# Decode attention with a squared-ReLU MLP: w1 loaded after the last V, some w2 rows on five DMA engines, wo in mid-step

## The chip, the cores and the metric

The kernel runs on one core of a Trainium2 chip. The time is device microseconds of one execution; 8 runs of the kernel before have a median of 137.36 us.

## The reference

Two tokens (one of each of two sequences) pass in parallel through an attention over the last 2048 positions of a cache and through an MLP; both results are added to the input. All arrays are bf16.

```python
# B=2, Sq=1, D=576, Hq=32, Hkv=16, Sk=8192, Dh=128, F=4608
def _A_ref(x, k_cache, v_cache, wq, wo):        # W = 2048, rep = 2
    q = (x @ wq).reshape(B, Sq, Hq, Dh).transpose(0, 2, 1, 3)
    k = jnp.repeat(k_cache[:, :, Sk - W:, :], rep, axis=1)
    v = jnp.repeat(v_cache[:, :, Sk - W:, :], rep, axis=1)
    scores = jnp.einsum("bhqd,bhkd->bhqk", q, k) * (Dh ** -0.5)
    o = jnp.einsum("bhqk,bhkd->bhqd", softmax(scores), v)
    return o.transpose(0, 2, 1, 3).reshape(B, Sq, Hq * Dh) @ wo

def _B_ref(x, w1, b1, w2, b2):
    h = x @ w1 + b1
    r = jnp.where(h > 0, h, 0)
    return (r * r) @ w2 + b2

xn = layernorm(x)
out = x + _A_ref(xn, ...) + _B_ref(xn, ...)
```

## The kernel before

**Units.** The attention is cut into NU = 8 units. A unit is one sequence and TH = 4 K/V heads, that is NC = 8 query heads. Its K is one tile of 128 partitions x 16 KB (2.1 MB), and so is its V. Units 2t and 2t+1 are the two sequences of head group t, of which there are NQ = 4.

**A step of a unit** (`step`): TensorE transposes K in NG = 8 groups of eight 128x128 blocks (`transposes`, L237); ScalarE and VectorE copy the groups to SBUF in turn (L240, L242); TensorE multiplies them with q (`scores`, L252). In the same loop go the products of the probabilities of the unit two back with its V (`pv`, L289). Then `softmax` works on VectorE, POOL and ScalarE: the maximum over columns and, by a reduction of POOL, over partitions, the exponential, the sums. When both units of a head group have their PV, `wo_proj` at the end of the step spreads the result (`rr`, on VectorE), gathers it with 8 selection matmuls (`wps`, L306), copies it (`ws`) and adds 16 matmuls with wo to the output sum `out_ps`, a PSUM tile that takes all contributions to the result (`out_acc`, L213: two matmuls of 288 columns for each row of weights).

**The MLP.** h is computed transposed: w1 is the stationary operand, 36 column chunks of 128 for each of KC = 5 row blocks (`mlp_h_block`, L323). The columns of a chunk are FR = 18 apart, so that w2 can be loaded with 18 whole rows of 1152 B behind each other on a partition. A bias and the square (L327, L331) give `hT_sb`; `mlp_o` multiplies it with one row of w2 per partition at a time into `out_ps`. Before, `mlp_h_block` runs in the steps of units 1 and 2, and `mlp_o` at the very end.

**Loads.** x comes over ScalarE's queue, b1 and b2 over POOL's (L146, L148), all else over SP's in the order in which the program lists it: wq with K0 between, k1, two tiles of w1, v0, k2, the rest of w1, v1, wo0, k3, then in turn V and K of later units with a wo tile for each head group, and last w2 in the five pieces of `W2P`, 9, 9, 9, 6 and 3 rows. K, V and w2 share a pool of six buffers (`kvpool`), so a load waits until what used the buffer six tiles earlier is done with it. w1 takes the four wide buffers of wq; wo has two buffers. `out_ps` is opened with x and b2 ahead of all other matmuls but the transposes.

**The end.** After the last piece of w2, `out_ps` is copied (L414) and stored from SP and ScalarE.

Of the kernel before, what the change touches and what calls it, by code (L numbers as in the profile page):

```python
# [9 lines left out]
BF16 = mybir.dt.bfloat16  # L10
# [6 lines left out]
def kernel(  # L17
# [43 lines left out]
    FR = L1 // P  # L61
    NFC = S * FR
    OH = D // 2
# [47 lines left out]

    def w_operands(tiles, c, col0, L, step=1):
        last = col0 + (P - 1) * step
        if c < NFULL:
            return tiles[c][:, col0:last + 1:step], c
        sg = col0 // L
        assert last // L == sg
        return tiles[c][:, col0 - sg * L:last - sg * L + 1:step], NFULL + sg
# [6 lines left out]

    def issue_w2(s, r0, r1):
        tl = kvpool.tile([P, (r1 - r0) * D], BF16, tag="kv", name=f"w2_{s}_{r0}")
        rows = B_w2[s * L1:(s + 1) * L1, :].rearrange("(p r) n -> p (r n)", r=FR)
        nc.sync.dma_start(out=tl[:], in_=rows[:, r0 * D:r1 * D])
        w2_tiles[(s, r0)] = tl  # L130

    x_sb = const.tile([B, D], BF16, name="x_sb")
# [10 lines left out]
    for c in range(2, KC):  # L143
        issue_wq(c)
    b1_sb = const.tile([P, S, FR], BF16, name="b1_sb")
    nc.gpsimd.dma_start(out=b1_sb[:], in_=B_b1.rearrange("(s p r) -> p s r", s=S, p=P))  # L146
    b2_sb = const.tile([1, D], BF16, name="b2_sb")
    nc.gpsimd.dma_start(out=b2_sb[:], in_=B_b2.rearrange("(o n) -> o n", o=1))  # L148

    ones_f = const.tile([P, P], F32, name="ones_f")  # L150
# [60 lines left out]
    def out_acc(lhsT, rhs_of, start=False, stop=False):  # L211
        for i in range(2):
            nc.tensor.matmul(out_ps[32 * i:32 * i + B, :], lhsT=lhsT, rhs=rhs_of(i * OH, (i + 1) * OH),  # L213
                             start=start, stop=stop, skip_group_check=True)

    out_acc(ident[:B, :B], lambda a, z: x_sb[:, a:z], start=True)
    out_acc(ones_b[:, :], lambda a, z: b2_sb[:, a:z])

# [77 lines left out]

    def wo_proj(tq):
        oG = oG_tiles.pop(tq)
# [9 lines left out]
        ws = work.tile([P, WR, B], BF16, tag="ws", name=f"ws_{tq}")  # L308
        nc.vector.tensor_copy(out=ws[:], in_=wps[:])  # L309
        wo_sb = wo_tiles.pop(tq)  # L310
        for r in range(WR):
# [4 lines left out]
    def mlp_h_block(c):  # L316
        if c == 0:
            mlp["ps"] = psum.tile([P, NFC, B], F32, tag="misc", bufs=2, name="hT_ps")
        hT_ps = mlp["ps"]
        for s in range(S):  # L320
            for r in range(FR):
                lhsT, xc = w_operands(w1_tiles, c, s * L1 + r, L1, FR)
                nc.tensor.matmul(hT_ps[:, s * FR + r, :], lhsT=lhsT, rhs=xnT[:, xc, :],  # L323
                                 start=(c == 0 and s == 0 and r == 0), stop=(c == KC - 1), skip_group_check=True)
        if c == KC - 1:
            t1 = work.tile([P, NFC, B], F32, tag="t1", name="t1")
            nc.vector.tensor_tensor(out=t1[:], in0=hT_ps[:],  # L327
                                    in1=b1_sb[:].rearrange("p s r -> p (s r)").unsqueeze(2).to_broadcast([P, NFC, B]),
                                    op=ALU.add)
# [5 lines left out]
    def mlp_o(s, r0, r1, last=False):  # L335
        w2_sb = w2_tiles.pop((s, r0))
        for r in range(r0, r1):
            o = (r - r0) * D
            out_acc(mlp["h"][:, s * FR + r, :], lambda a, z: w2_sb[:, o + a:o + z], stop=(last and r == r1 - 1))

    def load_k(u):
        for f in issue_kv(k_tiles, A_k_cache, u, "k"):
            f()

    def load_v(u):
        for f in issue_kv(v_tiles, A_v_cache, u, "v"):
            f()

    W2P = [(0, 0, 9), (0, 9, 18), (1, 0, 9), (1, 9, 15), (1, 15, 18)]

    load_k(1)
    issue_w1(0)
    issue_w1(1)
    load_v(0)
    load_k(2)
    for c in range(2, KC):
        issue_w1(c)
    load_v(1)
    issue_wo(0)
    load_k(3)  # L360
    nxt = {0: [], 1: [], 2: [lambda: load_v(2), lambda: load_k(4)]}

    def step(u, extra=()):
        for g in range(NG + 2):
            if g < NG:
                transposes(u, g)
            if u >= 1 and 1 <= g <= NG:
                if u >= 2:
                    pv(u - 2, g - 1)
            if g >= 2:  # L370
                scores(u, g - 2)
        softmax(u)

# [10 lines left out]
    softmax(0)  # L384
    step(1)
    mlp_h_block(0)
    mlp_h_block(1)
    for u in range(2, NU + 2):
        if u < NU:
            step(u)  # L390
        else:
            for g in range(NG):
                pv(u - 2, g)
        if u == 2:
            for c in range(2, KC):
                mlp_h_block(c)
        if u - 2 >= 1 and (u - 2) % B == B - 1:
            wo_proj((u - 2) // B)
        if u < NU:
            load_v(u)  # L400
            if u % B == 0:
                issue_wo(u // B)
            if u + 2 < NU:
                load_k(u + 2)
        if u >= NU - 1:
            pass
        if u == NU - 1:
            for w in W2P:
                issue_w2(*w)
    for i, w in enumerate(W2P):  # L410
        mlp_o(*w, last=(i == len(W2P) - 1))

# [34 lines left out]
```

## Time and profile before

| | |
|---|---|
| median of 8 runs | 137.36 us (137.16 to 137.5) |
| the profiled execution | 137.44 us, span of its instructions 135.6 us |
| TensorE matmuls, weight loads | busy 101.2 us (75%), 92.2 us (68%), 2054 of each |
| VectorE, ScalarE, POOL | busy 53.8, 43.0, 10.0 us |
| mean granted TensorE clock | 0.786 of full |
| read from HBM | 53.62 MB, 395 GB/s over the span |
| K transposes | 512 matmuls, 264 ns listed each |
| scores, PV | 512 each, 168 and 167 ns listed |
| h, 36 chunks x 5 blocks | 180 matmuls, 201 ns listed |

A busy share is the time in which an engine has an instruction in hand. TensorE's matmuls overlap, so the listed time of one is longer than the distance to the next, and the share says little about how close it is to its limit. The line of tenths for DMA gives the mean share of the 16 DMA engines that were moving data in each fortieth of the span. A wait is put down to what ended it last.

### The profile page before, as it was taken

What the parts mean: (1) busy time and instruction counts of PE and PEld (TensorE: products, weight loads), DVE (VectorE), ACT (ScalarE), POOL (GpSimd) and SP (SyncE); (2) the same over time, 40 slices, a digit from 0 to 9 for tenths busy, and PEclk for the clock granted to TensorE, in tenths of its full rate; (3) what the DMA queues carried; (4) which work ended last, traced back from release to release, by engine and by line L of the source; (5) the groups of instructions that cost most, each with busy time, mean ns of one, the idle gap of its engine ahead of it and who ended that gap; (6) DMA issues with size and microseconds to landing.
All of it is one profiled execution on the core that took longest, in us unless ns stands there. A gap on an engine that the chain in (4) does not pass through costs nothing.

```text
span 135.6 us, 4461 instructions
## 1 busy us (share of the span) xinstructions
PE 101.2 (75%) x2054; PEld 92.2 (68%) x2054; DVE 53.8 (40%) x124; ACT 43.0 (32%) x47; POOL 10.0 (7%) x31
## 2 busy tenths in 40 slices
PE   1049928599968999679943995998399599768661
PEld 0039927589968999639943994798399489754430
DVE  7502511574352433502553446365544654650001
ACT  6704730165013801005601550362155137110000
POOL 6400000110110001100011001101100110110000
PEclk9999995559955995555995599599559959955999
DMA  4999999999999999999999999999999999999940
GB/s 109 423 421 425 423 435 413 417 440 421 430 404 419 440 413 413 441 425 408 437 425 430 416 435 420 410 435 425 430 430 413 437 411 427 413 416 413 390 161 1
DMA packets 5278, 53.90 MB, mean 397 GB/s; under 512 B 630, under 2 KB 652, under 8 KB 1164
## 3 DMA queue, kind: packets, MB, share of 16 engines
q1 hardware_dynamic: 5188, 53.61, 94.6%
q8 instruction: 16, 0.26, 0.8%
q0 software_dynamic: 64, 0.01, 0.1%
q14 instruction: 2, 0.02, 0.0%
q10 hardware_dynamic: 8, 0.00, 0.0%
HBM read 53.62 MB, written 0.00 MB: 395 GB/s over the span
## 4 chain that ended last, share of the span: by engine, by line
DMA 70%; PE 23%; issue 1%; DVE 1%; POOL 1%; ACT 1%; POOLq 0%; ACTq 0%
DMA k<-in_A_k_cache_dram 44%; DMA w<-in_B_w_dram 22%; PE kT_ps L237 14%; DMA b_sb<-in_B_b_dram 4%; PE sc_ps L252 3%; PE oT_ps L289 3%; PE out_ps L213 2%; PE qT_ps L225 1%; ACT kT L240 1%; POOL b_sb L146 1%; DVE sub L266 1%; DVE fin_sb L414 0%; POOL gmax L262 0%; PE pro_ps L186 0%; DVE gm L264 0%
## 5 line engine op out<-in xcount | busy, mean ns | idle before, releaser
L237 PE MATMUL kT_ps<-ident,k 128*128 128x128 bf16 x512 | 48.6, 264 | 10.2 <-DMA k<-in_A_k_cache_dram 10.0
L237 PEld LDWEIGHTS <-k 128*128 128x128 bf16 x512 | 40.5, 121 | 12.1 <-DMA k<-in_A_k_cache_dram 10.9
L240 ACT COPY kT<-kT_ps 128x1024 bf16<-128x1024 bf16 x32 | 32.3, 1012 | 40.0 <-PE kT_ps L237 40.0
L242 DVE COPY kT<-kT_ps 128x1024 bf16<-128x1024 bf16 x32 | 22.1, 690 | 33.1 <-PE kT_ps L237 33.1
L252 PE MATMUL sc_ps<-qT_all,kT 128*128 128x8 bf16 x512 | 21.7, 168 | 1.3 <-ACT kT L240 0.6
L252 PEld LDWEIGHTS <-kT 128*128 128x128 bf16 x512 | 19.4, 101 | 2.1 <-ACT kT L240 0.8
L289 PE MATMUL oT_ps<-pT,v 128*128 128x8 bf16 x512 | 15.4, 167 | 1.5 <-ACT pT L269 0.9
L269 ACT ACTIVATE pT<-sub 128x512 bf16<-128x512 f32 x8 | 5.0, 630 | 35.3 <-DVE sub L266 35.3
L289 PEld LDWEIGHTS <-v 128*128 128x128 bf16 x512 | 14.4, 99 | 1.7 <-DMA v<-in_A_v_cache_dram 0.9
L271 DVE TENSOR_REDUCE l<-pT 128x8 f32<-128x512 bf16 x8 | 8.5, 1064 | 4.5 <-ACT pT L269 4.5
L323 PE MATMUL hT_ps<-xnT,w 128*128 128x2 bf16 x144 | 9.8, 201 | 0.0
L323 PEld LDWEIGHTS <-w 128*128 128x128 bf16 x144 | 9.4, 167 | 0.0
L258 DVE TENSOR_REDUCE m<-sc_ps 128x8 f32<-128x512 f32 x8 | 5.5, 691 | 9.7 <-PE sc_ps L252 9.7
L262 POOL PARTITION_ALL_REDUCE gmax<-m x8 | 2.9, 365 | 84.9 <-DVE m L260 84.9
L213 PE MATMUL out_ps<-wo,ws 128*2 128x288 bf16 x64 | 7.2, 392 | 2.4 <-DVE ws L309 2.4
L213 PE MATMUL out_ps<-w,hT_sb 128*2 128x288 bf16 x72 | 5.7, 308 | 2.4 <-DMA w<-in_B_w_dram 2.4
L213 PEld LDWEIGHTS <-hT_sb 128*2 128x2 bf16 x72 | 3.4, 91 | 4.8 <-issue 3.0
L213 PEld LDWEIGHTS <-ws 128*2 128x2 bf16 x64 | 3.1, 103 | 4.8 <-DVE ws L309 2.8
L225 PE MATMUL qT_ps<-xnT,wq 128*128 128x2 bf16 x128 | 3.9, 164 | 2.8 <-DMA wq<-in_A_wq_dram 2.5
L225 PEld LDWEIGHTS <-wq 128*128 128x128 bf16 x128 | 3.7, 99 | 2.8 <-DMA wq<-in_A_wq_dram 2.6
L266 DVE TENSOR_TENSOR sub<-sc_ps,gm 128x512 f32<-128x512 f32 x8 | 5.5, 690 | 0.3
L273 POOL PARTITION_ALL_REDUCE lsum<-l x8 | 3.2, 398 | 24.5 <-DVE l L271 24.5
(58 smaller groups left out, 35.3 us busy)
## 6 DMA issues: line engine op xcount, KB each, us to landing
v<-in_A_v_cache_dram SPq DMA_DIRECT2D x8, 2048.0 KB, 28.5
k<-in_A_k_cache_dram SPq DMA_DIRECT2D x7, 2048.0 KB, 29.4
w<-in_B_w_dram SPq DMA_DIRECT2D x4, 1152.0 KB, 17.6
wo<-in_A_wo_dram SPq DMA_DIRECT2D x4, 1152.0 KB, 27.3
wq<-in_A_wq_dram SPq DMA_DIRECT2D x4, 1024.0 KB, 7.0
w<-in_B_w_dram SPq DMA_DIRECT2D x3, 1296.0 KB, 22.3
k<-in_A_k_cache_dram SPq DMA_DIRECT2D x2, 1024.0 KB, 9.1
w<-in_B_w_dram SPq DMA_DIRECT2D x1, 864.0 KB, 15.7
```

Of the source, the lines that this page charges most:

```text
L213: nc.tensor.matmul(out_ps[32 * i:32 * i + B, :], lhsT=lhsT, rhs=rhs_of(i * OH, (i + 1) * OH), start=start, stop=stop, skip_group_check=True)
L225: nc.tensor.matmul(qT_ps[:, h, :], lhsT=lhsT, rhs=xnT[:, xc, :], start=(c == 0 and h == 0), stop=(c == KC - 1), skip_group_check=True)
L237: nc.tensor.transpose(out=kT_ps[:, i * P:(i + 1) * P], in_=k_sb[:, j * Dh:(j + 1) * Dh], identity=ident[:])
L240: nc.scalar.copy(out=kT[:], in_=kT_ps[:])
L242: nc.vector.tensor_copy(out=kT[:], in_=kT_ps[:])
L252: nc.tensor.matmul(sc_ps[:, g * JG + i, :], lhsT=kT[:, i * P:(i + 1) * P], rhs=qT_all[:, b, tq * NC:(tq + 1) * NC], start=True, stop=True)
L258: nc.vector.tensor_reduce(out=m1[:], in_=sc_ps[:].rearrange("p j c -> p c j"), axis=AX.X, op=ALU.max)
L266: nc.vector.tensor_tensor(out=sub[:], in0=sc_ps[:], in1=gm2[:].unsqueeze(1).to_broadcast([P, NJ, NC]), op=ALU.subtract)
L269: nc.scalar.activation(out=pT[:], in_=sub[:], func=ACT.Exp, scale=scale)
L271: nc.vector.tensor_reduce(out=l1[:], in_=pT[:].rearrange("p j c -> p c j"), axis=AX.X, op=ALU.add)
L289: nc.tensor.matmul(oT_ps[:], lhsT=v_sb[:, j * Dh:(j + 1) * Dh], rhs=pT_tiles[u][:, j, :], start=(j == 0), stop=(j == NJ - 1))
L323: nc.tensor.matmul(hT_ps[:, s * FR + r, :], lhsT=lhsT, rhs=xnT[:, xc, :], start=(c == 0 and s == 0 and r == 0), stop=(c == KC - 1), skip_g ...
```

## The change

- `FT`, `FX`, `CH`: the second half of w2's rows is no longer 18 rows on each of 128 partitions. 16 rows on each stay so (2048 rows); 240 rows go to a tile of 20 partitions x 12 rows, `w2x_sb`, and 16 rows to a tile of 16 partitions x 1 row, `w2y_sb`. h has 47 chunks in place of 36: 34 of 128 columns, 12 of 20 and one of 16. `hT_ps` is set to zero first.
- `issue_w2x`: `w2x_sb` is loaded by four loads of five partitions (13,824 B each), one after another of the first four among the loads v1, k3, v2, k4, with `w2y_sb` behind the fourth.
- b1 is loaded in four parts into a zeroed tile, b1 and b2 are issued on POOL after unit 0's softmax, and x and b2 are added to `out_ps` after step 1.
- Order of SP's loads from k1 on: v0, k2, v1, wo0, k3, v2, k4, wo1, v3, k5, v4, k6, v5, k7, wo2, v6, v7, w1 (two tiles), wo3, w1 (three tiles), w2.
- `wo_proj` is cut into `wo_sel` and `wo_acc`. For head groups 0 and 1 they run inside the steps of units 4 and 6, at groups 3 and 6. For the last two they run between the PVs of the last units and the h blocks.
- All of h is computed after the last PV, then the 13 rows of `w2x_sb` and `w2y_sb` (`mlp_x`), then w2 in pieces of 9, 9, 9, 4, 2 and 1 rows.

```diff
+    XR, XP, XE = 12, 20, 5
+    FT = (L1 - XR * XP) // P
+    FX = L1 - FT * P
+    XQ = FX - XR * XP
+    FX0 = L1 + FT * P
+    CH = [(r, FR, P) for r in range(FR)] + [(L1 + r, FT, P) for r in range(FT)]
+    CH += [(FX0 + r, XR, XP) for r in range(XR)] + [(FX0 + XR * XP, 1, XQ)]
+    NFC = len(CH)
...
+        nr = FT if s else FR
         tl = kvpool.tile([P, (r1 - r0) * D], BF16, tag="kv", name=f"w2_{s}_{r0}")
-        rows = B_w2[s * L1:(s + 1) * L1, :].rearrange("(p r) n -> p (r n)", r=FR)
+        rows = B_w2[s * L1:s * L1 + nr * P, :].rearrange("(p r) n -> p (r n)", r=nr)
...
+    w2x_sb = const.tile([XP, XR * D], BF16, name="w2x_sb")
+    w2y_sb = const.tile([XQ, D], BF16, name="w2y_sb")
+    x_parts = list(range(XP // XE))
+
+    def issue_w2x():
+        if x_parts:
+            i = x_parts.pop(0)
+            rows = B_w2[FX0:FX0 + XR * XP, :].rearrange("(e i r) n -> i e (r n)", e=XE, r=XR)
+            nc.sync.dma_start(out=w2x_sb[i:XP:XP // XE, :], in_=rows[i])
+            if not x_parts:
+                nc.sync.dma_start(out=w2y_sb[:], in_=B_w2[FX0 + XR * XP:F, :])
...
-    def wo_proj(tq):
+    wo_state = {}
+
+    def wo_sel(tq):
...
+        wo_state[tq] = ws
+
+    def wo_acc(tq):
+        ws = wo_state.pop(tq)
         wo_sb = wo_tiles.pop(tq)
...
+            nc.vector.memset(mlp["ps"][:], 0.0)
         hT_ps = mlp["ps"]
...
+        for i, (f0, step, m) in enumerate(CH):
+            lhsT, xc = w_operands(w1_tiles, c, f0, L1, step, m)
+            nc.tensor.matmul(hT_ps[0:m, i, :], lhsT=lhsT, rhs=xnT[:, xc, :],
+                             start=(c == 0 and i == 0), stop=(c == KC - 1), skip_group_check=True)
...
+    def mlp_x():
+        for i, (f0, step, m) in enumerate(CH[FR + FT:]):
+            w = w2x_sb[0:m, i * D:(i + 1) * D] if m == XP else w2y_sb[:]
+            out_acc(mlp["h"][0:m, FR + FT + i, :], lambda a, z: w[:, a:z])
+
     def load_k(u):
...
+        if u >= 3:
+            issue_w2x()
 
     def load_v(u):
...
+        if u >= 1:
+            issue_w2x()
+
+    W2P = [(0, 0, 9), (0, 9, 18), (1, 0, 9), (1, 9, 13), (1, 13, 15), (1, 15, 16)]
 
     load_k(1)
-    issue_w1(0)
-    issue_w1(1)
     load_v(0)
     load_k(2)
-    for c in range(2, KC):
-        issue_w1(c)
     load_v(1)
     issue_wo(0)
     load_k(3)
...
-    step(1)
+    load_v(2)
+    b1_sb = const.tile([P, NFC], BF16, name="b1_sb")
+    nc.gpsimd.memset(b1_sb[:], 0.0)
+    o = 0
+    for f0, n, m in ((0, FR, P), (L1, FT, P), (FX0, XR, XP), (FX0 + XR * XP, 1, XQ)):
+        nc.gpsimd.dma_start(out=b1_sb[0:m, o:o + n], in_=B_b1[f0:f0 + n * m].rearrange("(p r) -> p r", r=n))
+        o += n
+    b2_sb = const.tile([1, D], BF16, name="b2_sb")
+    nc.gpsimd.dma_start(out=b2_sb[:], in_=B_b2.rearrange("(o n) -> o n", o=1))
+    step(1, {})
+    load_k(4)
+    issue_wo(1)
+    out_acc(ident[:B, :B], lambda a, z: x_sb[:, a:z], start=True)
+    out_acc(ones_b[:, :], lambda a, z: b2_sb[:, a:z])
+    for u in range(2, NU):
+        hooks = {}
+        if u >= 4 and u % B == 0:
+            hooks = {3: [lambda t=u // B - 2: wo_sel(t)], 6: [lambda t=u // B - 2: wo_acc(t)]}
+        step(u, hooks)
+        if u + 1 < NU - 1:
+            load_v(u + 1)
+        if u + 3 < NU:
+            load_k(u + 3)
+        if u == 4:
+            issue_wo(2)
+        if u == 5:
+            load_v(NU - 1)
+            issue_w1(0)
+            issue_w1(1)
+        if u == 6:
+            issue_wo(3)
+            for c in range(2, KC):
+                issue_w1(c)
+            for w in W2P[:2]:
+                issue_w2(*w)
+    for w in W2P[2:4]:
+        issue_w2(*w)
+    for g in range(NG):
+        pv(NU - 2, g)
+    issue_w2(*W2P[4])
+    wo_sel(NQ - 2)
+    wo_acc(NQ - 2)
+    for g in range(NG):
+        pv(NU - 1, g)
+    issue_w2(*W2P[5])
     mlp_h_block(0)
     mlp_h_block(1)
...
+    wo_sel(NQ - 1)
+    wo_acc(NQ - 1)
+    for c in range(2, KC):
+        mlp_h_block(c)
+    mlp_x()
+    for i in range(len(W2P)):
+        mlp_o(*W2P[i], last=(i == len(W2P) - 1))
```

## The prediction

> **What bounds the kernel now.** I read the busy slices and the DMA queues of the page first, because a kernel that reads 53.6 MB for two tokens is most likely bound by its loads.
>
> ```profile
> DMA  4999999999999999999999999999999999999940
> ...
> q1 hardware_dynamic: 5188, 53.61, 94.6%
> q8 instruction: 16, 0.26, 0.8%
> ```
>
> The 16 DMA engines are full in nearly every slice, and queue q1, which holds all the loads that SP issues, is 94.6% of what they do. The q8 line will matter: 16 packets of 16 KB, which carry instructions. The table by stage shows where the engines stop being full.
>
> ```profile
> core 0: us, PE busy (x) PEld busy (x) DVE busy (x) ACT busy (x) POOL busy (x), PEclk, DMA share, GB/s
> ...
> 60.00:90.00 30.00, 23.91 (x469) 22.23 (x466) 13.12 (x26) 11.38 (x12) 1.53 (x4) 0.75 1.01 424
> 90.00:119.00 29.00, 23.87 (x546) 22.46 (x544) 15.15 (x32) 11.38 (x12) 1.89 (x5) 0.82 1.01 423
> 119.00:128.00 9.00, 7.08 (x124) 4.84 (x125) 2.04 (x7) 0.63 (x1) 0.40 (x1) 0.62 1.00 414
> 128.00:129.50 1.50, 0.34 (x6) 0.26 (x7) 0.00 (x0) 0.00 (x0) 0.00 (x0) 1.00 0.72 293
> 129.50:131.40 1.90, 1.08 (x20) 0.63 (x16) 0.00 (x0) 0.00 (x0) 0.00 (x0) 1.00 0.50 189
> 131.40:132.00 0.60, 0.60 (x12) 0.41 (x9) 0.00 (x0) 0.00 (x0) 0.00 (x0) 1.00 0.12 46
> ```
>
> The DMA share is 1.0 until 128 us. Then it is 0.50 for 1.9 us: **half of the engines have nothing left, the other half still work.** The packet records of the trace say the same. The last piece of w2 is marked done by eight engines between 128.2 and 129.5, and by the other eight between 131.4 and 131.8. Following each engine from load to load by the moments of its marks, I see it lose about 1.55 us at once when one of the 16 instruction packets falls on it. They fall on eight engines in turn, twice each: 2 x 1.55 = 3.1 us, the gap between the groups. The late eight set the end. The timeline shows what is behind them.
>
> ```profile
> 131.25 0.90 PE L213 MATMUL out_ps<-w,hT_sb 128*2 128x288 bf16 x12 [0.82 <-DMA w<-in_B_w_dram]
> ...
> 132.34 0.53 PE L213 MATMUL out_ps<-w,hT_sb 128*2 128x288 bf16 x6 [0.18 <-DMA w<-in_B_w_dram]
> ...
> 132.91 0.45 DVE L414 CAST fin_sb<-out_ps 34x288 bf16<-34x288 f32 x1 [10.06 <-PE out_ps L213]
> 133.38 0.32 SPq L415 DMA_DIRECT2D out_dram<-fin_sb  x1
> ```
>
> The last w2 piece lands at 132.3 us, its three rows take 0.53 us, then come a copy and the store. Only two things can move the end: when the last engine is done, and how much TensorE work follows the last landing.
>
> [...] The kernel before has only 128-row loads on SP, so its trace doesn't test the case of five. [...]
>
> **The change, part by part.**
>
> *Rows of w2 on five engines.* 256 of the rows leave the even split: 256 x 1152 B / 16 = 18,432 B less on each engine. The load of 16 rows puts 1,152 B back: 17,280 B less. At 424 GB/s (stage 60 to 90 us), 26.5 GB/s an engine, that is **-0.65 us**[...]. The other 240 rows, 276,480 B, come in four loads of five partitions: 55,296 B[...], net +38,016 B, **+1.43 us** there.
>
> *Smaller pieces.* The last w2 loads go from 6 and 3 rows to 4, 2 and 1: nine more packets per engine, counting the 16-row load. In the packet records 6912 B took 264 ns and 3456 B 139 ns, which leaves some 10 ns a packet beyond the bytes: +0.09 us. b1 comes in four small loads in place of one. Before, one packet of 576 B per engine took some 40 ns, and its mark 9 ns; three more loads and their marks are 0.05 to 0.15 us, I take +0.10.
>
> *The tail.* One row follows the last landing in place of three. The trace has the rows of this stage 122 ns apart at full clock: two rows less are **-0.24 us**, if TensorE is waiting for that landing and its clock is up (at half clock rows are 240 ns apart, as before 126.0 us, and the single row costs 0.12 more).
>
> *w1 behind the last V.* The bytes are the same, so this costs nothing as long as the queue never runs dry and TensorE is done with everything else when the last pieces land. K and V of a unit are 4.19 MB, 9.9 us at 424 GB/s. TensorE's step of unit 6, from its K at 97.2 to its last PV at 106.3, took 9.1 us, so it keeps up by 0.8 us a unit. Behind k7 there will be wo2, v6, v7, w1, wo3 and w2, 16.9 MB: k7 lands 40 us before the end of the stream, at about 92, and v7 at about 104.5. Scores and softmax of unit 7 (4.7 us from first reduction to reciprocal, at 116.7 to 121.4 before) let PV of unit 7 end near 107. The one-row load waits for that, since it takes v7's buffer, and its turn comes near 130: 20 us of cover.
>
> The h blocks are tighter. By the bytes behind them, w1's third and fourth tiles land at 115.8 and 118.6, its rest at 120.0, the three w2 pieces of nine rows at 123.1, 126.3 and 129.4, the last row at 131.8. In the trace the h matmuls start 62 ns apart at either clock; the 13 new chunks have 20 or 16 columns in place of 128, and I price them at the 27 ns of wq's matmuls (32 in 0.79 to 0.99 us). A block is 34 x 62 + 13 x 27 ns = 2.5 us, the last ends at 123.5, bias and square at 124.1. Then come 47 rows. They start at half clock, since the clock stood at 0.5 through the h blocks at 51 to 54 us. It rose after 3.1 us of rows before (122.9 to 126.0); its changes lie 3.4 us or a multiple apart, so 1.9 to 5.3 us until it rises are possible. All rows together take 47 x 0.122 + 0.49 x that time: without any waiting they end between 130.8 and 132.4, at 131.6 in the middle. The landing allows 132.0. **The cover is 0.4 us in the middle case, and -0.4 in the worst**; I take 0.
>
> *Work moved or added elsewhere, taken at zero.* The 55 more matmuls for h and 22 more for the output, in that reckoning already, are 154 more instructions with their weight loads[...]. wo in mid-step removes waits of about 2 us each (1.1 for rr, 1.0 for ws) from TensorE, which then waits for K instead. The last two wo projections lie between 104 and 114 us, before w1 is complete. The new VectorE memset (0.30 us for out_ps) lies there too. POOL gets a memset and five loads at 0.56 to 1.02 us behind the sum of softmax 0; the next POOL work, the maximum of unit 1, comes after a K that lands at 25.8 us and a step. b2 may land near 37 us, with step 2 of TensorE queued behind its matmul, whose K comes at about 36: a delay of a microsecond, which the 0.8 us a unit and the buffers take up. SP issues five more loads at about 0.4 us each. In the trace an SP load from the ninth on never goes out before the eighth ahead of it has landed (v1 at 25.83, k1 at 25.82). Counting that in the new order, at least 5.4 MB, 12.7 us, stay in flight.
>
> **The sum**: late engines -0.65 + 0.09 + 0.10 = -0.46; tail -0.24; together -0.70. The profiled execution took 137.44 us (span 135.60 and 1.84 around it), so 136.74; the median of the runs is 0.08 lower: **136.7**. The five engines end at 128.2 to 129.5 plus 1.62, at most 131.1; the late ones at 131.8 - 0.46 = 131.3. They still set the end, if the five are free ones.
>
> [...] No record bears an engine's number. [...] I take three in four for free.
>
> **The rivals.** *A hit engine is among the five* (0.16, slower). Its mark, 131.4 to 131.8, moves by 1.43 + 0.19 to 133.0 to 133.4, 1.2 to 1.6 later than the latest before; less the tail, +1.0 to +1.4: about 138.5. It decides from the point where one of the five had a mark before above 130.4, and all of the late group do. *TensorE is late for the last pieces* (0.14): a late rise of the clock costs 0.4; if the narrow chunks take 62 ns too, blocks of 2.9 us follow each other without a gap from 115.8 and end 1.0 later; both together +1.4. That gives 137.1 to 138.1, middle 137.5: from faster through none to slower. Against it stands the middle case's cover. *The small loads go to all engines* (0.06, no difference): then tail and packets remain, -0.24 + 0.19, 137.3.
>
> **How the numbers follow.** Forecast 0.64, all of it faster; rivals 0.16, 0.14, 0.06. What a measurement of this kernel can tell from no change is about 0.2%, 0.27 us. Of the late TensorE I count 0.05 faster, 0.04 same, 0.05 slower: faster 0.69, same 0.10, slower 0.21. The bounds of the forecast's terms give 136.4 to 137.0. Idle time of the early eight is worth at most 8 x 3 / 16 = 1.5 us with full levelling, which with the tail would be 135.6; I set the low end at 136.0 for a part of that. The high end, 138.0, takes in the second and third rivals and leaves out the first, which with some low cases is under 2 in 10.
>
> **What will show it.** In the profile after: a share of the DMA engines above 0.8 until a microsecond before the last landing (right), or a stretch near 0.3 or less with a few at work (the first rival); the last w2 landing at about 131.8; two matmuls after it; TensorE waiting for w2 before the last pieces (if it never waits, the second rival); DMA share at 1.0 from 2 to 128 us, or the queue ran dry. I am wrong on the main step if the last landing doesn't come earlier than 132.3.

## The result and the profile after

The changed kernel takes 143.14 us (median of 11 runs, 141.02 to 145.58) where the kernel before takes 137.37: the ratio is 1.0347, with an interval of 1.0322 to 1.0372. By that ratio it is slower by 4.8 us, where 0.7 us less was forecast. Medians here and below are of all runs, while ratios, and differences between kernels, compare the runs within 1.5% of the fastest of their kernel (for the changed kernel five of them, median 142.28 us, for e17 only two). The changed kernel scatters far more than the kernel before, which keeps to 137.2 to 137.6 at clocks from 0.74 to 0.79. Its profiled execution is the longest of all (146.17 us, span 144.1) and has the lowest mean TensorE clock, 0.692, so its times late in the span are a bad case; e7 below has the same instructions in a profile of 141.38 us.

The busy slices and DMA queues of the page, after:

```profile
PEclk9999975579655555955985557975896555555569
DMA  4999999999999999999999999999999999992000
...
q1 hardware_dynamic: 5404, 53.61, 88.9%
q8 instruction: 16, 0.26, 0.7%
```

The loads did what was forecast. There are again 16 instruction packets. The last w2 load gives 16 landing signals in both profiles (between its two groups of eight before, the DMA share is 0.50, so each is read as one engine's): before, eight came from 128.9 to 129.9 us and eight from 131.9 to 132.29; after, three came from 128.2 to 128.9 and thirteen from 130.0 to 131.85. But for three engines the two groups have closed up, and the last landing is 0.44 us earlier. But the row of tenths has three empty slices behind it: for some 12 us the kernel runs on with no load left. The table by stage (engine columns in the order PE, PEld, DVE, ACT, POOL, then PEclk, DMA share, GB/s) shows who runs:

```profile
114.00:131.00 17.00, 16.00 (x259) 15.15 (x258) 1.01 (x5) 0.00 (x0) 0.00 (x0) 0.50 0.96 397
131.00:134.30 3.30, 3.25 (x28) 1.49 (x30) 0.00 (x0) 0.00 (x0) 0.00 (x0) 0.50 0.02 8
134.30:141.20 6.90, 6.88 (x70) 3.85 (x68) 0.00 (x0) 0.00 (x0) 0.00 (x0) 0.62 0.00 0
```

TensorE is busy with hardly a pause, at half clock nearly throughout. Its timeline from the last PVs on, after:

```profile
104.70 1.75 PE L301 MATMUL oT_ps<-pT,v 128*128 128x8 bf16 x64
106.30 0.35 PE L320 MATMUL wps<-rr,sel 128*128 128x16 bf16 x8
109.94 2.08 PE L228 MATMUL out_ps<-wo,ws 128*2 128x288 bf16 x16 [3.28 <-DVE ws L323]
111.96 1.87 PE L301 MATMUL oT_ps<-pT,v 128*128 128x8 bf16 x64
...
114.62 5.51 PE L341 MATMUL hT_ps<-xnT,w 128*128 128x2 bf16 x92
...
127.58 2.83 PE L341 MATMUL hT_ps<-xnT,w_rem 128*128 128x2 bf16 x47
131.05 3.04 PE L228 MATMUL out_ps<-w2x_sb,hT_sb 20*2 20x288 bf16 x24 [0.64 <-DVE hT_sb L349]
133.89 0.44 PE L228 MATMUL out_ps<-w2y_sb,hT_sb 16*2 16x288 bf16 x2
134.26 6.92 PE L228 MATMUL out_ps<-w,hT_sb 128*2 128x288 bf16 x68
```

Before, the three last groups of rows each waited for w2; two of them stand in the prediction, and this is the first:

```profile
129.16 1.27 PE L213 MATMUL out_ps<-w,hT_sb 128*2 128x288 bf16 x18 [1.40 <-DMA w<-in_B_w_dram]
```

After, no row waits for any load: **TensorE sets the end, by itself.** Two things stand out. The first is the wait of 3.28 us ahead of the rows of wo 2, with PV of unit 7 queued behind it. VectorE's timeline says what the copy `ws` was waiting for:

```profile
104.88 0.69 DVE L270 TENSOR_REDUCE m<-sc_ps 128x8 f32<-128x512 f32 x1 [0.45 <-PE sc_ps L264]
...
107.92 1.05 DVE L283 TENSOR_REDUCE l<-pT 128x8 f32<-128x512 bf16 x1 [0.69 <-ACT pT L281]
109.57 0.20 DVE L287 RECIPROCAL rinv<-lsum 128x8 f32<-128x8 f32 x1 [0.60 <-POOL lsum L285]
109.69 0.12 DVE L306 TENSOR_TENSOR oG<-oT_ps,rinv 128x8 bf16<-128x8 f32 x1
109.72 0.16 DVE L323 CAST ws<-wps 128x16 bf16<-128x16 f32 x1
```

The copy takes 0.16 us, but it stands behind the whole softmax of unit 7, with its waits for POOL and ScalarE. It is not the only one: `ws` of wo 0, in step 4, waits behind softmax 3 in the same way, for 3.62 us. The second is that 13 narrow rows (20 or 16 partitions) run at 0.24 us each, and that the clock rises only at 139.6 us, 8.5 us after the first row.

### The profile page after: what moved, and what is told of

Read it like the earlier page. It is cut to its first block, busy times and chain, and to the rows that moved or that the text cites. A ratio compares the mean times of both kernels' runs of the same rounds, so it can differ in the third digit from the quotient of the medians.

```text
span 144.1 us, 4625 instructions
## 1 busy us (share of the span) xinstructions
PE 112.6 (78%) x2131; PEld 99.4 (69%) x2131; DVE 53.2 (37%) x125; ACT 42.4 (29%) x47; POOL 11.4 (8%) x35
## 4 chain that ended last, share of the span: by engine, by line
PE 56%; DVE 16%; DMA 12%; ACT 5%; issue 4%; POOL 3%; SPq 2%; POOLq 0%; ACTq 0%
PE kT_ps L249 18%; PE out_ps L228 13%; DMA wq_rem<-in_A_wq_dram 12%; PE hT_ps L341 9%; PE sc_ps L264 9%; PE oT_ps L301 6%; DVE l L283 4%; DVE sub L278 3%; ACT pT L281 3%; ACT kT L252 2%; DVE kT L254 2%; DVE m L270 2%; POOL gmax L274 2%; SPq L107 1%; POOL lsum L285 1%
## 5 line engine op out<-in xcount | busy, mean ns | idle before, releaser
L249 PE MATMUL kT_ps<-ident,k 128*128 128x128 bf16 x512 | 51.3, 272 | 3.8 <-DMA k<-in_A_k_cache_dram 2.4
L249 PEld LDWEIGHTS <-k 128*128 128x128 bf16 x512 | 42.1, 124 | 4.2 <-DMA k<-in_A_k_cache_dram 2.5
L254 DVE COPY kT<-kT_ps 128x1024 bf16<-128x1024 bf16 x32 | 21.6, 682 | 24.0 <-PE kT_ps L249 24.0
L301 PE MATMUL oT_ps<-pT,v 128*128 128x8 bf16 x512 | 16.2, 167 | 1.2 <-issue 1.2
L228 PE MATMUL out_ps<-wo,ws 128*2 128x288 bf16 x64 | 8.4, 439 | 6.9 <-DVE ws L323 6.9
L341 PEld LDWEIGHTS <-w 128*128 128x128 bf16 (+2 forms) x188 | 10.9, 153 | 0.6 <-issue 0.5
L341 PE MATMUL hT_ps<-xnT,w 128*128 128x2 bf16 (+2 forms) x188 | 11.2, 194 | 0.0
L228 PEld LDWEIGHTS <-ws 128*2 128x2 bf16 x64 | 4.1, 115 | 9.2 <-DVE ws L323 7.1
L228 PEld LDWEIGHTS <-hT_sb 128*2 128x2 bf16 (+2 forms) x94 | 5.3, 112 | 5.2 <-DVE hT_sb L349 0.7
L228 PE MATMUL out_ps<-w,hT_sb 128*2 128x288 bf16 x68 | 6.9, 388 | 0.0
```

The source lines that it names most:

```text
L249: nc.tensor.transpose(out=kT_ps[:, i * P:(i + 1) * P], in_=k_sb[:, j * Dh:(j + 1) * Dh], identity=ident[:])
L254: nc.vector.tensor_copy(out=kT[:], in_=kT_ps[:])
L301: nc.tensor.matmul(oT_ps[:], lhsT=v_sb[:, j * Dh:(j + 1) * Dh], rhs=pT_tiles[u][:, j, :], start=(j == 0), stop=(j == NJ - 1))
L341: nc.tensor.matmul(hT_ps[0:m, i, :], lhsT=lhsT, rhs=xnT[:, xc, :], start=(c == 0 and i == 0), stop=(c == KC - 1), skip_group_check=True)
```

## The experiments

The first four kernels weigh these causes: that w1 behind the last V makes TensorE late (A in the texts below), that the split of w2 costs the time (B), that wo in mid-step does it (C), and that VectorE holds the attention up (e3). Where a cut shows only lines that were added, the same lines are gone from their old places.

**e1: the changed kernel with w1 early.** The loads of w1 and the h blocks go back to the places that they have before.

```diff
     load_k(1)
+    issue_w1(0)
+    issue_w1(1)
     load_v(0)
...
+    mlp_h_block(0)
+    mlp_h_block(1)
     for u in range(2, NU):
```

> The changed kernel, with the w1 loads and the five h blocks back at their places of the kernel before; all else as changed. Theory A (TensorE is left with h and the rows of w2 behind the last PV, at half clock): 136.5 to 137.2 us, TensorE waits for w2 at the end again. Theory B (the split of w2 into 47 chunks and the five-engine loads cost the time): 140 or more. Theory C (wo in mid-step stalls TensorE): 139 to 141.

143.94 us, median of four runs from 140.78 to 144.68. Theory A had 136.5 to 137.2, and even the lowest run is far above, though 14 us of h matmuls have left the end: they delay the steps instead, and PV of unit 7 ends at 125.6 us (113.8 after). The narrow rows begin at 128.8, the clock rises at 137.3. Late w1 is not the cause.

**e2: the kernel before with w1 late**, and nothing else of the change.

```diff
         if u == NU - 1:
+            for c in range(KC):
+                issue_w1(c)
             for w in W2P:
                 issue_w2(*w)
...
+    for c in range(KC):
+        mlp_h_block(c)
     for i, w in enumerate(W2P):
```

> The kernel before, with only the w1 loads moved behind the last V and the five h blocks behind the last wo projection; 36 chunks, wo_proj at step ends and the old pieces of w2. Theory A: 139.5 to 142 us, since 180 h matmuls at 60 ns (10.8 us) and 36 rows at 0.24 us (8.6 us) follow a last PV that ends near 112 us. Theories B and C: 137.4, as before.

137.32 us, ratio 1.000 (0.9991 to 1.0009): no difference. TensorE's timeline, end:

```profile
107.27 2.01 PE L289 MATMUL oT_ps<-pT,v 128*128 128x8 bf16 x64 [1.50 <-ACT pT L269]
...
112.51 9.09 PE L323 MATMUL hT_ps<-xnT,w 128*128 128x2 bf16 x144
...
124.42 3.84 PE L213 MATMUL out_ps<-w,hT_sb 128*2 128x288 bf16 x36 [0.59 <-DVE hT_sb L331]
129.16 1.27 PE L213 MATMUL out_ps<-w,hT_sb 128*2 128x288 bf16 x18 [0.89 <-DMA w<-in_B_w_dram]
```

PV of unit 7 ends at 109.3, the h blocks run from 112.5, and the rows still wait for the last three pieces: 0.89, 0.81 and 0.18 us, 1.9 in all, where the kernel before waited 1.40, 0.82 and 0.18, 2.4 in all. So w1 late is covered, and costs half a microsecond of TensorE's reserve at the end.

**e3: one more copy of K on ScalarE** for each unit of the changed kernel (`g % 2 == 0 or g == 1`), which takes 4.6 us off VectorE.

> The changed kernel, with the second of the eight K copies of each unit on ScalarE in place of VectorE, so that the next unit's first copies don't stand behind softmax on VectorE. If softmax on VectorE paces the attention once K comes earlier: the last PV ends 1 to 3 us earlier and the time is 1 to 3 us less (139 to 141). If K's landing paces it, or only the work behind the last PV counts: no difference (142).

141.09 us, ratio 1.0277 (1.0218 to 1.0336). By the ratios about 1 us of the loss goes, and the intervals of the two kernels still touch. PV of unit 7 ends at 110.0; the wait for `ws` behind softmax 7 stays at 3.29 us.

**e4: wo 0 and 1 at the ends of steps 3 and 5** in place of mid-step.

> The changed kernel, with the wo projections of head groups 0 and 1 at the ends of the steps of units 3 and 5, as before. Theory C: under 139 us. Theory A: 1 to 2 us less than the changed kernel (140 to 141), by the 3.6 us wait for ws ahead of unit 4 and its like, of which only a part comes back.

144.78 us, ratio 1.054 (1.0524 to 1.0557): worse by 2.7 us than the changed kernel. The mid-step place of these two is not what costs; wo 2, which stayed, still waits 3.26 us between the last two PVs.

From this came a second theory, **T** in the texts below: TensorE's work after the last PV is too long, because wo 2 stands in front of PV 7 and because the w2 split adds work that runs at half clock.

**e5: the kernel before with the w2 split alone** (47 chunks, five-partition loads, last pieces of 4, 2 and 1 rows). The narrow rows are multiplied after step 4.

> The kernel before with only the w2 split: 47 chunks, the 256 rows in five-partition loads, last pieces of 9, 9, 9, 4, 2 and 1 rows. w1, the h blocks and wo stay where they were, and the 13 narrow rows are multiplied after step 4, far from the end. If the DMA arithmetic of the prediction was right and only TensorE's tail was overlooked (theory T), this is the predicted gain by itself: -0.7 us, 136.5 to 136.9, ratio 0.995, last w2 mark near 131.3, TensorE waiting for the last pieces. If the five-engine loads do harm by themselves (the first rival), a group of marks ends near 133 and the time is 138 to 139. If the split only ever costs TensorE time in a place that matters, no place of it is at the end here, and nothing above 137.4 is expected.

139.35 us, ratio 1.0109 (1.0073 to 1.0146), slower, where T expected a gain. The last mark (a packet of 4 B that takes 9 ns, behind the data of a load; before, the last one ends at 131.80 us, and the last landing signal comes at 132.29) is at 131.19, as T said, but TensorE isn't waiting for it: PV of unit 7 ends at 127.0 (121.6 before). The narrow rows after step 4 stand in front of PV of unit 3, whose `rr` queues behind softmax 4 on VectorE; TensorE waits 1.93 us for it. The narrow rows are not the reason, though: e16 below has that wait without them.

**e6: wo 2 in step 7**, ahead of softmax 7, in the changed kernel.

```diff
+        if u == NU - 1:
+            hooks = {NG + 1: [lambda: wo_sel(NQ - 2), lambda: wo_acc(NQ - 2)]}
         step(u, hooks)
...
-    wo_sel(NQ - 2)
-    wo_acc(NQ - 2)
```

> The changed kernel with the selection and rows of wo 2 in step 7, ahead of softmax 7, in place of between PV of unit 6 and PV of unit 7. Theory T: PV of unit 7 no longer stands behind a copy that queues behind softmax 7; it ends near 110 in place of 113.8, all that follows on TensorE moves by the same, -3 to -3.5 us against the changed kernel at equal clock: 139 to 140, ratio 1.01 to 1.02. If the order of wo 2 is harmless because TensorE would wait for softmax 7 anyway: PV of unit 7 ends later than 112, and the time stays within 1.5 us of the changed kernel, 141.5 to 143.

139.89 us, ratio 1.0179 (1.0162 to 1.0196), in the range that T gave, and by the ratios 2.3 us less than the changed kernel (T had 3 to 3.5). TensorE's timeline:

```profile
105.66 1.27 PE L301 MATMUL oT_ps<-pT,v 128*128 128x8 bf16 x45 [0.83 <-ACT pT L281]
107.22 0.62 PE L301 MATMUL oT_ps<-pT,v 128*128 128x8 bf16 x19 [0.29 <-issue]
...
125.08 3.04 PE L228 MATMUL out_ps<-w2x_sb,hT_sb 20*2 20x288 bf16 x24 [0.64 <-DVE hT_sb L349]
...
128.29 6.07 PE L228 MATMUL out_ps<-w,hT_sb 128*2 128x288 bf16 x68
```

PV of unit 7 ends at 107.8, and everything behind it has moved up. What is left of the loss stands in the last two lines: rows from 125.08 to 134.4 us, with no wait, and the clock at half until 131.9.

**e7: the narrow rows behind the third w2 piece** in the changed kernel, the same instructions in another order.

> The changed kernel with the 13 narrow rows (20 or 16 partitions) multiplied behind the three pieces of nine rows in place of ahead of them; the same instructions in another order. If narrow rows do not count towards the rise of the clock (theory T), the clock rises 1.9 to 5.3 us after the first full row, so up to 3.2 us earlier by the clock on the wall, and the narrow rows run at 0.12 us in place of 0.24: -1.5 to -2 us, 141 to 141.5. If they count as well as full rows and the clock had just been late, no difference (within 0.5 us of 143.1).

140.94 us, ratio 1.0182 (1.0148 to 1.0216), some 2 us less than the changed kernel, with four runs from 139.33 to 143.05.

```profile
109.46 1.87 PE L301 MATMUL oT_ps<-pT,v 128*128 128x8 bf16 x64
...
128.57 5.18 PE L228 MATMUL out_ps<-w,hT_sb 128*2 128x288 bf16 x54 [0.64 <-DVE hT_sb L349]
133.69 1.63 PE L228 MATMUL out_ps<-w2x_sb,hT_sb 20*2 20x288 bf16 x24
```

Full rows begin at 128.57 and the clock rises 3.5 us later; the narrow rows then take 1.63 us where they took 3.04. All rows together take 7.8 us, 10.1 after. **The traces fit narrow rows that do not bring the clock up.** Counted from the first narrow row, the clock rose after 8.5 us (after), 8.5 (e1), 7.3 (e3), 5.7 (e4) and 6.8 (e6); counted from the first full row behind them, after 5.3, 5.3, 4.1, 2.5 and 3.6. Where full rows came first it rose after 3.1 us (before and e2), 3.5 (e7) and 4.1 (e8). It is not proof, since the rise was late in two kernels without narrow rows: after 5.9 us in e12, and after 9.6 in e11, with pauses of 0.15 and 0.87 us between its rows.

**e8: the changed kernel without the split** (36 chunks, pieces of 5, 3 and 1 rows).

> The changed kernel with w2 undivided as before: 36 chunks, last pieces of 5, 3 and 1 rows, no five-engine loads, no narrow rows. wo in mid-step and w1 behind the last V stay. Theory T: 55 h matmuls of 60 ns (3.3 us) and 11 rows (13 narrow less 2 full, 2.6 us at half clock) leave TensorE's tail, so it has caught up with the loads by the last piece or nearly so: 137.3 to 139, ratio 1.00 to 1.012. If the place of wo alone makes the loss, nearly all of it stays: 141 or more.

137.62 us, ratio 1.0023 (1.0011 to 1.0034).

```profile
106.99 1.87 PE L285 MATMUL oT_ps<-pT,v 128*128 128x8 bf16 x64
...
123.65 4.46 PE L212 MATMUL out_ps<-w,hT_sb 128*2 128x288 bf16 x36 [0.59 <-DVE hT_sb L333]
129.16 1.27 PE L212 MATMUL out_ps<-w,hT_sb 128*2 128x288 bf16 x18 [1.04 <-DMA w<-in_B_w_dram]
130.89 0.78 PE L212 MATMUL out_ps<-w,hT_sb 128*2 128x288 bf16 x10 [0.47 <-DMA w<-in_B_w_dram]
131.97 0.67 PE L212 MATMUL out_ps<-w,hT_sb 128*2 128x288 bf16 x8 [0.31 <-DMA w<-in_B_w_dram]
```

The late groups of rows wait for w2 again: the loads set the end, although wo 2 still waits 3.29 us ahead of PV 7 here. By the ratios, the split carries 4.5 of the 4.8 us. A part of that lies ahead of h: PV of unit 7 ends at 108.9 us here and at 111.3 in e7, at mean clocks of 0.770 and 0.778.

**e10 and e11: what the small pieces and the order of wo 2 are worth where the loads set the end.** e10 is the kernel before with pieces of 5, 3 and 1 rows at the end of w2; e11 is e8 with wo 2 in step 7.

> The kernel before with the last three w2 pieces of 9 (6 and 3 before) cut into 5, 3 and 1 rows, nothing else. The prediction's tail term alone: -0.24 us less 0.05 for the packets, 137.1 to 137.3, ratio 0.9985. If the last two pieces land together, because the late engines finish the 3 rows and the 1 row 0.35 us apart and TensorE takes the 3 rows in 0.36: no difference, 137.3 to 137.5.

> The changed kernel with both suspects taken out: w2 undivided (36 chunks) and wo 2 in step 7 ahead of softmax 7. wo 0 and 1 in mid-step and w1 behind the last V stay. Theory T: TensorE is 2 to 3 us ahead of where it was without the split, waits for the last w2 pieces in every run, and the loads alone set the end: 137.1 to 137.4, ratio 0.998 to 1.000. If something else of the change costs too (b1 and b2 loads, the memset, w1 late): above 137.6.

e10 takes 137.16 us, ratio 0.9983 (0.9977 to 0.999): the tail term alone, -0.2 us, and the fastest kernel here. e11 takes 137.61, ratio 1.0018 (1.001 to 1.0026), 0.2 above what was expected. It is as long as e8: what the order of wo 2 was worth in e6 is worth nothing once TensorE has to wait for loads. PV of unit 7 ends at 106.0 in its profile, and the gain goes into waits, of which these are two:

```profile
104.24 1.77 PE L285 MATMUL oT_ps<-pT,v 128*128 128x8 bf16 x64 [1.74 <-DMA v<-in_A_v_cache_dram]
...
109.81 2.40 PE L325 MATMUL hT_ps<-xnT,w 128*128 128x2 bf16 x36 [0.40 <-DMA w<-in_B_w_dram]
```

The 0.2 us lie outside the span of its instructions: that is 135.56 us on average, as in the kernel before (135.55), but there are 2.05 us around it in place of 1.82. The kernels made from the changed one have 2.03 to 2.18, and so have e13 and e16; e5 and e17, with the whole split, have 1.8. What makes the difference stays open.

**e9 and e12: the five engines' share without narrow chunks.** Partitions 112 to 127 of 13 w2 rows come in loads of 5, 5, 5 and 1 partitions, partitions 0 to 111 in one; TensorE's work stays as before. e9 does this in the kernel before, e12 in the changed kernel with the mends of e6 and e8.

> The kernel before, with part of w2 given to the five engines in a way that adds no TensorE work: all 36 chunks keep 128 rows; for 13 of the rows in the free dimension, partitions 112 to 127 come in three loads of five partitions and one of one partition, early, and the other 112 partitions in one load. 208 rows of w2 leave the even split (before the changed kernel: 256), and the last pieces are of 5, 3 and 1 rows. If the DMA arithmetic of the prediction holds and only TensorE's extra work spoiled it (theory T): -0.57 us at the late engines, up to -0.24 for the tail, 136.6 to 137.0, ratio 0.994 to 0.997, last marks near 131.3. If five-engine loads bring nothing by themselves: 137.3 to 137.5.

> The changed kernel with wo 2 in step 7, and the five-engine share taken from full chunks as in e9 (208 rows, no narrow chunk, no added TensorE work). Theory T: DMA ends 0.57 us earlier than in e11 and nothing on TensorE hides it: 136.5 to 136.9, the fastest of all. If TensorE then sets the end again because w1 is late and the clock rises late: 137.2 to 138.

148.39 us (ratio 1.0795) and 148.87 (1.0825). The table by stage of e9:

```profile
122.00:126.00 4.00, 0.77 (x23) 0.60 (x20) 2.28 (x5) 0.63 (x1) 0.76 (x2) 0.50 0.99 213
126.00:128.00 2.00, 0.47 (x17) 0.47 (x18) 0.00 (x0) 0.00 (x0) 0.00 (x0) 0.50 1.00 200
```

The engines are "busy" (share 0.99 and 1.00) and move half of what they did. Packets of 14,976 B took 1105 ns (median) in the load of 112 partitions, and 560 to 565 for the fastest in the small loads. So a full DMA share doesn't mean full bandwidth, and these two say nothing on the forecast's term.

**e13, e16, e17: the split's loads with TensorE's work of before (e13, e16), or whole but with the narrow rows late (e17).** e13 is e5 less 11 of the 13 narrow chunks, so it leaves 216 rows of w2 out of the output, and e16 leaves out the same; e16 puts the two that are left behind the third w2 piece; e17 does that with all 13.

> The kernel of e5 (the kernel before with the w2 split alone), with 11 of the 13 narrow chunks left out of the computation: all loads stay as they are, but TensorE does 36 chunks and 36 rows, as before. It leaves 216 of the rows of w2, and their columns of w1, out of the output. If the extra TensorE work alone spoils the split (theory T): the loads set the end again, -0.46 to -0.7 us, 136.6 to 136.9, ratio 0.995. If five-engine loads cost something else as well: 137.3 or more.

> e13 (all loads of the split, TensorE's 36 chunks and 36 rows as before, 11 narrow chunks left out of the output) with its two narrow rows behind the third w2 piece in place of after step 4. In e13 TensorE never waited for w2 and ended 3 us later than before with the same work: the rows after step 4 had pushed PV of unit 3 behind softmax 4, and the selection behind it waited 1.9 us. If that order was all that hid the gain: TensorE waits for the last w2 pieces again, the last marks near 131.3 set the end, 136.6 to 136.9, ratio 0.995. If the five-engine loads cost by themselves: 137.3 or more with TensorE waiting at the end.

> e5 (the kernel before with the w2 split alone, everything computed) with the 13 narrow rows behind the third w2 piece in place of after step 4: -0.7 us at the loads, against 55 more h matmuls at 45 to 60 ns in steps 1 and 2 (2.5 to 3.3 us, beside waits for K of 10 us in all) and 11 more rows at the end at full clock (1.3 us, beside waits for w2 of 2.4 us). If the waits cover them: 136.6 to 137.0 and the fastest kernel of all. If the clock rises late or the h blocks push the steps: 137.5 to 138.5.

138.34 us (1.0035, 1.0017 to 1.0054), 138.06 (1.0041, 1.0009 to 1.0073) and 141.21 (1.0145, 1.0101 to 1.0189). All three miss. The runs of e13 reach from 137.11 to 140.47; in seven of the 22 the span of the instructions is 135.1 to 135.3 us, shorter than any of the kernel before (135.4 to 135.9), but none of these was profiled. The text for e16 gives e5's wait of 1.9 us to e13, where it was 3.74. e16's timeline of TensorE has the reason, against the second line, which is the kernel before's:

```profile
87.21 0.36 PE L331 MATMUL wps<-rr,sel 128*128 128x16 bf16 x8 [3.52 <-DVE rr L325]
```

```profile
83.34 0.35 PE L306 MATMUL wps<-rr,sel 128*128 128x16 bf16 x8 [0.59 <-DVE rr L300]
```

With the split's loads in the program, the order on TensorE changes elsewhere: PV of units 2 and 3 stands behind all scores of the next unit in place of between them, so the selection of wo 1 waits for a VectorE that is in softmax 4. It comes 3.9 us later, and TensorE is 2.1 us later at the last PV (123.7 against 121.6). Of e16's 0.56 us, 0.3 are in the span of the instructions (136.0 us on average, 135.7 before), and the rest lies outside it. The last marks of e16 and e17 are at 131.65 and 131.59, and TensorE's rows follow each other to the end without a wait.

**e14, e15, e18: what slowed e9.** e14 takes every eighth partition in the small loads, and the rest in loads of 16 partitions eight apart. e15 and e18 are e13 with other destinations for its four small loads; the source of e18's loads, and of e15's first two, is that of e13.

> e9 with other partitions in its loads, the same 208 rows: partitions 7, 15, 23 and so on (every eighth) come in three loads of five and one of one, and the other 112 in seven loads of 16 partitions, each eight apart. In e9, packets of 14,976 B took 565 ns alone, but 886 to 1181 ns when five engines wrote partitions next to each other at once, and 1105 ns in the load of 112 partitions, and the 16,384 B packets beside them 1190 ns in place of 614. If neighbouring partitions from different engines are what slows them: 565 to 580 ns here, 425 GB/s throughout, time 136.6 to 137.0. If the tile or the size of the packets is the cause: still 1000 ns or more, and 145 to 149 us.

> e13 with its four small loads of five partitions in four kinds, one each: destination partitions four apart, source rows 55 KB apart; destination neighbouring, source 55 KB apart; both neighbouring (source rows 13.8 KB apart); destination four apart, source neighbouring. The two narrow rows that are multiplied read other data than in e13, so what is left out is the same plus these. If the destination decides: packets of 13,824 B take 524 ns in the first and fourth load and 800 ns or more in the second and third. If the source decides: slow in the third and fourth. If neither: 524 ns in all, and e9's slowness comes from something else, such as the tile's place.

> e15 again, all four loads with the same source as in e13 and partitions four apart; only the first partition differs: 32, 64, 36 and 3. [...] packets of 13,824 B at 518 to 525 ns in the first and fourth load, 560 ns and more in the second and third, with the packets beside them slowed, and two of e15's four losses of some 0.5 us each. If closeness to partitions 0 to 19 or anything else decides: not this pattern. The same rows are left out of the output as in e15.

e14: 144.69 us (1.0546), packets of 14,976 B up to 1165 ns. e15: 141.24 us, all four loads slow (up to 629, 1013, 749 and 862 ns), the first of them too, which has e13's source and writes partitions 20 to 36 in steps of four. So neither nearness nor the source alone decides. e18, 138.97 us: 518 to 525 ns in the first load, up to 806 in the second, up to 900 in the third, 518 to 524 with one of 568 in the fourth. In the second and third not every packet is slow: three of the ten took 525 or 526 ns. From 59 to 61.5 us, around the second load, the stream moved 311 GB/s at a DMA share of 1.04; from 72 to 77 us, around the fourth, 427 at 1.02. The size of the packets and the step of four partitions are the same in all four, and the sources and the places in the stream are those of e13, whose loads begin at partitions 0, 1, 2 and 3, as in the changed kernel (516 to 525 ns in both; in the last of the four up to 554 after and 605 in e13). What differs is the first partition: 32 and 3 were fast, 64 and 36 slow. So the packets fit the pattern that was expected for e18; why those partitions are slow is not shown, since no record says which engine carried a packet. One run of each of e15 and e18 is all there is.

## Why the prediction was wrong

**The loads: right.** Forecast were -0.46 us at the late engines, with ends at 131.3, and the five engines of the small loads free of instruction packets. Over ten profiles with the split (after, e1, e3 to e7, e13, e16, e17) the last mark lies at 131.08 to 131.65, mean 131.36; over five without it (before, e2, e8, e10, e11) at 131.78 to 131.85, mean 131.81. The difference is -0.45. No group of marks came at 133, so the first rival is out. Of the eight engines that were early before, three are early after, which fits five engines of the free group with more bytes to carry; the three in four that the forecast gave to this was the author's estimate. That a load of five partitions is carried by five engines was an assumption of the forecast, which counted 55,296 B on each of them. The profile after has 20 packets of 13,824 B in four groups of five, and in the first two groups all five start within 0.13 us (from 38.45 and 46.65 us) and take 516 to 524 ns, so five are under way at once. Which five engines they are, no record says.

**The tail: right in size.** -0.24 was forecast, e10 has -0.2.

**The step that failed is TensorE's cover behind w1 late: "The cover is 0.4 us in the middle case, and -0.4 in the worst", taken as 0.** TensorE was to end its rows at 131.6 us, ahead of the loads. In the profile after it ends them at 141.2, in e7's at 136.4, and never waits for w2. Three terms of that sum were mis-sized.

1. *"wo in mid-step removes waits", taken at zero, and "PV of unit 7 end near 107".* The four wo projections made TensorE wait 5.4 us in all before, not 2 each, and 7.5 after (lines below). PV of unit 7 ends at 113.8 in the profile after, and at 107.8 in e6, where wo 2 stands ahead of softmax 7. That this is near the forecast is in part luck, since wo 0 waits in e6 too (3.63 us). The forecast listed the matmuls that move, but not what the 0.16 us copy queues behind: for a moved step the queue of each engine that it uses has to be walked. In e7, with the same order as after and a clock nearer to e6's, PV ends at 111.3: the order of wo 2 costs 3.5 us, and the other 2.5 of the 6 are the slower execution of the one profile.
2. *Narrow chunks at 27 ns.* In the last block of the profile after, starts are 62 ns apart for full chunks (201 ns listed each), 37 for narrow ones (163 to 178 listed), with a gap of 131 ns where the width changes: 46 ns each for the 13. That is 1.2 us more in five blocks. The rival's 62 was wrong too.
3. *"so 1.9 to 5.3 us until it rises are possible".* This was the author's estimate, from one rise after 3.1 us and steps of 3.4 us. The steps stand in both profiles (each recorded stretch of one clock but the cut-off last one is 3.41 us or a multiple, up to 30.7); that 1.9 us can be enough, no trace shows. With the 13 narrow rows first in line it took 5.7 to 8.5 us. They ran at half clock for 3.2 us without a rise. In e6 the half clock lasted 6.8 us of rows in place of the 3.4 of the middle case; at the forecast's 0.49 us for each us, that is 1.7.

These are the waits of the first term, before (two lines) and after (two lines):

```profile
PE wps L306 <- DVE rr L300: 3.0, 4, 1.1
PE out_ps L213 <- DVE ws L309: 2.4, 4, 1.0
...
PE out_ps L228 <- DVE ws L323: 6.9, 2, 3.6
PE wps L320 <- DVE rr L314: 0.6, 1, 0.6
```

The 6.9 us are wo 2's 3.28 and wo 0's 3.62. The latter stands in the first line here; the second is the same place in e8, without the split and without a wait:

```profile
63.33 2.08 PE L228 MATMUL out_ps<-wo,ws 128*2 128x288 bf16 x16 [3.62 <-DVE ws L323]
...
56.98 1.15 PE L212 MATMUL out_ps<-wo,ws 128*2 128x288 bf16 x16
```

With the order of wo 2 mended (e6), the second and third terms are what is left: rows start at 125.08 where 124.1 was forecast, and take 9.3 us where 7.4 was. They end at 134.4 in place of 131.6. These 2.8 us, and the 0.2 more that lie outside the span, are about what e6's 139.89 us exceeds the forecast by, 3.2. The second rival, TensorE late for the last pieces, named the mechanism, with "a late rise of the clock" and dearer chunks; it had 0.14 and +1.4 us.

**What hid the gain.** TensorE waited 2.4 us for w2 before, at a mean clock of 0.786, and that was all its reserve. The split adds 2.4 us of h (15.8 us from the first h to the last after, 13.4 in e8) and 11 rows, 1.3 us at full clock and 2.6 at half. It also comes with another order of PV on TensorE, which makes TensorE wait for VectorE (wo 0 in the changed kernel, wo 1 in e16). In no place that was tried did 0.45 us at the loads pay for this: early it delays the steps (e1, e5), late it is the end (after, e6, e7). With the added work gone (e16) a loss of 0.4% is left, of the order and of the time outside the span. A kernel with the split's loads, before's work and before's order was not made, so that 0.7 us would then come is argued: the marks alone point to it.

**w1 late costs nothing by itself** (e2), as forecast. It takes 0.5 us of the reserve of 2.4.

What stays open is how the 4.8 us divide: e6 gives 2.3 to the order of wo 2, e7 some 2 to the narrow rows' place and e8 4.5 to the split, and these overlap, since each gain is worth something only until the loads set the end.

## What to carry to other kernels

A kernel bound by loads can have a second engine close behind: before taking a load off, count that engine's reserve in waits at the very end (2.4 us here), and price the added instructions there, at the clock that they will run at. When a step moves, walk every engine's queue at its new place: a copy of 0.16 us behind a softmax made TensorE wait 3.3. Where a small load gives some DMA engines more bytes than others, time its packets at several destination partitions: the same 13,824 B took 518 to 525 ns from partition 32 on, and up to 900 from 36 on (e18). A DMA share of 1.0 doesn't show packets that take twice as long (e9: 200 GB/s where 424 were moved before, and 1105 ns in place of 565 for 14,976 B); the column of GB/s does.

## What the hardware showed that was not expected

- Matmuls of 20 or 16 partitions by 288 columns took as long as full ones, 0.24 us a row at half clock and 0.12 at full, and seem not to bring the clock up. Nor did h matmuls of two columns: after, the clock stood at 0.5 from 114 to 131 us, through 13.7 us of them with 2.1 us of wo rows between.
- A small load can slow the loads beside it, in e15's first two and in e18 by its destination partitions alone: in e15, each load of 69 KB cost the stream 0.4 to 0.9 us against e13 (335 to 368 GB/s in the stretches around the four), with 9,216 B packets at up to 860 ns in place of 351.
- The runs of kernels in which TensorE sets the end scatter (after 141.0 to 145.6, e13 137.1 to 140.5), those of the kernel before do not (137.2 to 137.8). The mean clock goes with it only loosely: the changed kernel took 141.38 us at 0.767 and 145.49 at 0.762.
